# Adding an attention mask on VectorE instead of by a product on TensorE, from unit 12 of 24 on

## The chip, the cores and the metric

The kernel runs on one core of a Trainium2 chip. The metric is the time of one execution on the device in microseconds; a profiled execution also gives the span, from the first to the last instruction of the core. The engines are named as the profile names them: PE (TensorE, with its weight loads as PEld), DVE (VectorE), ACT (ScalarE), POOL (GpSimd) and SP (SyncE, which issues the transfers here).

## The reference

Three parts follow each other: a sparse attention, and two feed-forward layers on its output. All inputs and outputs are float32.

```python
def _attn_ref(q, k, v):                       # (2, 8, 768, 64) each
    k_sum = k.reshape(B, H, nb, 32, D).max(axis=3)
    v_sum = v.reshape(B, H, nb, 32, D).mean(axis=3)
    scores_l = scale * np.matmul(q, k.transpose(0, 1, 3, 2))
    mask_l = np.abs(pos[:, None] - pos[None, :]) < 16
    scores_s = scale * np.einsum('bhsd,bhnd->bhsn', q, k_sum) + np.log(32)
    scores_all = np.concatenate([np.where(mask_l, scores_l, -1e9), scores_s], axis=-1)
    a = softmax(scores_all)                   # written out, with 1e-9 in the divisor
    return np.matmul(a, np.concatenate([v, v_sum], axis=2))

def reference(...):
    x = attention, laid out as 1536 tokens x 512
    h = x @ w_in                              # 512 -> 2048
    x = (h * sigmoid(1.702 * h)) @ w_out      # 2048 -> 512
    return (sigmoid(x @ w_gate) * (x @ w_val)) @ w_out2   # 512 -> 1536 -> 512
```

Each token attends to the 31 tokens around it and to 24 block summaries; every other score is masked away.

## The kernel before

**Attention.** The work is cut into 24 units: 2 batches, 3 groups of four query blocks of 64 tokens, 4 pairs of heads. A unit's scores are a tile of 128 x 4 x 128: the rows are two heads by 64 queries, and each of the four blocks has 128 columns, of which the first 32 are block summaries and the other 96 the window. For unit `u`, `w_copy` scales the keys on POOL; `b_pe` (L553) fills one of three PSUM banks `ps_s` with first one product of `pick` and `mask` (L557, bf16, 512 columns), which lays the mask into the bank, and then four products of keys and queries (L559) accumulated on it; `b_max` (L562) takes the negated maximum of each block on VectorE (L564); `b_exp` (L567) makes four exponentials on ScalarE out of the bank into an SBUF tile `e`, with their sums. Then follow `n_inv` and `n_mul` (the division, VectorE and POOL), `c_pe` (four transposes of `e` into the bank `ps_p`, L592), `c_copy` (`pt`, out of that bank, L597, on ScalarE for the first ten units and on VectorE after them), `d_pe` (products with the values, L611), and `d_hi` and `d_lo`, which split the result into a high and a low float32r part. The pool of `e` has three buffers, that of `ps_s` three banks, `ps_p` one.

**Loop.** Step `t` of the loop at L703 issues `b_pe`, `b_max` and `b_exp` of unit `t`, `n_inv` and `n_mul` of unit `t - 1`, and `c_pe`, `c_copy` and `d_pe` of unit `t - 3`, in the order of the list `ORDER` (L638). Between them it issues transfers, sums for the second batch (`sum_v`, L521), pieces of weight decoding (`pull`, L102 to L112) and pieces of the first feed-forward layer for the tokens that are ready (`filler`). That layer has products into `ps_h`, a sigmoid on ScalarE (L373), a gating product on VectorE (L364), the split of its result into `gh` (ScalarE, L365) and `gl` (POOL, L366), and products into `ps_o` (all L349), accumulated by L425 or L429.

**Order.** Only SP runs in the order that the program writes down (`manual_schedule`). For the other engines a planner, which lays out a timeline with costs of its own (`schedule_with_timeline_sim`), decides the order of each engine's instructions, preferring what stands earlier in the program among what it holds to be ready. The engines then run in that fixed order and wait where they must.

**After the attention.** The rest of the two layers is a long run of 128x512 products on PE.

Of the kernel before, what the change touches and what calls it, by code (L numbers as in the profile page):

```python
# [8 lines left out]
F32 = mybir.dt.float32  # L9
# [4 lines left out]
ALU = mybir.AluOpType  # L14
AX = mybir.AxisListType
PSUM = bass.MemoryType.PSUM
P = 128
# [11 lines left out]
def attention_moe_moe2_kernel(ctx: ExitStack, tc: tile.TileContext, ins: dict, out: bass.AP):  # L29
    nc = tc.nc  # L30
# [13 lines left out]
    G = 4  # L44
    NG = NQB // G
    NTT = S // P
    NSLOT = G + NG - 1
# [120 lines left out]
    def load(slots, layer, g, i):  # L168
        raw, shape = raws.pop(0)
        hi, lo = (slots.tile(list(shape), F32R, name=f"w{layer}_{g}_{i}{x}") for x in "HL")  # L170
        parts = decode(raw, hi.rearrange("p a n -> p (a n)"), lo.rearrange("p a n -> p (a n)"))
        for step, _ in enumerate(parts):
            if step == 1 and (layer, g) != (1, 0):
                fetch()
            yield
        return hi, lo

    def load_group(layer, g):
        tiles = weights[layer, g] = []
        ready[layer, g] = 0  # L180
        for i in range(len(mats[layer])):
            tiles += yield from load(w_slots, layer, g, i)
            ready[layer, g] += 1
            yield
# [256 lines left out]
    acc_b = None  # L441
    EARLY = 4
    EARLY_UNITS = 10
    coming = (x for n in range(2) for x in load_group(*groups[n]))

    def pull(n):
        for _ in range(n):
            if next(coming, True):
                break
# [5 lines left out]
    with tc.manual_schedule(engines={mybir.EngineType.SP}), ExitStack() as es:  # L455
        one = es.enter_context(tc.tile_pool(name="a_one", bufs=1))
# [4 lines left out]
        ep = es.enter_context(tc.tile_pool(name="a_e", bufs=3))  # L461
        vp = es.enter_context(tc.tile_pool(name="a_v", bufs=1))
        ps_a = es.enter_context(tc.tile_pool(name="ps_a", bufs=1, space=PSUM))

        vwin = one.tile([P, 2 * G, H * D], F32, name="vwin")
        mask = one.tile([P, NSLOT, P], BF16, name="mask")
        pick = one.tile([P, P], BF16, name="pick")

        units = [(b, g, hp) for b in range(B) for g in range(NG) for hp in range(HP)]
        qbd, vsum, kraw, kmax, kx = {}, {}, {}, {}, {}  # L470
# [8 lines left out]
        def load_q(u, eng):  # L479

            b, g, hp = units[u]
            t = qp.tile([P, G, P], F32, tag="q", name=f"q{u}")
            eng.dma_start(out=t.rearrange("p i c -> p (i c)"), in_=q[b, g, hp])
            qbd[u] = t
# [32 lines left out]
        def sum_v(b, hp):  # L517
            if hp == 0:
                vpart[b] = vp.tile([P, HP, W0], F32, tag="vm", name=f"vm{b}")
                nc.vector.memset(vpart[b], 0.0)  # L520
            nc.vector.tensor_reduce(  # L521
                out=vpart[b][:, hp, 0:NB], in_=vtl.pop((b, hp)).rearrange("p (n t) -> p n t", t=BLK),
                axis=AX.X, op=ALU.add,
            )

        def sum_lay(b):
            r = vpart.pop(b)
            ps = ps_a.tile([W0, H * D], F32, tag="x", name="ps_v", bufs=2)
            for hp in range(HP):
                nc.tensor.matmul(ps[:, hp * P:(hp + 1) * P], lhsT=r[:, hp], rhs=ident, start=True, stop=True)  # L530
            nc.scalar.activation(vsum[b][0:W0], ps, AF.Copy, scale=1.0 / BLK)

        def prep_k(b, hp):
            ks = kp.tile([P, W0], F32, tag="ks", name=f"ks{b}_{hp}")
            nc.vector.memset(ks, 0.0)
            own = kraw[b, hp][:, HALO:HALO + S].rearrange("p (n t) -> p n t", t=BLK)
            nc.vector.tensor_reduce(out=ks[:, 0:NB], in_=own, axis=AX.X, op=ALU.max)
            kmax[b, hp] = ks
# [11 lines left out]

        live = {}

        def b_pe(u):  # L553
            b, g, hp = units[u]
            t, kt = qbd.pop(u), kx.pop(u)
            ps = ps_a.tile([P, G, P], F32, tag="s", name="ps_s", bufs=3)
            nc.tensor.matmul(ps, lhsT=pick, rhs=mask[:, g:g + G, :], start=True, stop=False)  # L557
            for j in range(G):
                nc.tensor.matmul(ps[:, j, :], lhsT=t[:, j, :], rhs=kt[:, j, :], start=False, stop=j == G - 1)  # L559
            live["s", u] = ps  # L560

        def b_max(u):  # L562
            nm = sp.tile([P, G], F32, tag="nm", name="nm")
            nc.vector.tensor_reduce(out=nm, in_=live["s", u], axis=AX.X, op=ALU.max, negate=True)  # L564
            live["nm", u] = nm

        def b_exp(u):  # L567
            s, nm = live.pop(("s", u)), live.pop(("nm", u))
            sm = sp.tile([P, G], F32, tag="sm", name="sm")
            e = ep.tile([P, G, P], F32, tag="e", name="e")  # L570
            for j in range(G):
                nc.scalar.activation(  # L572
                    e[:, j, :], s[:, j, :], AF.Exp, bias=nm[:, j:j + 1], accum_out=sm[:, j:j + 1]
                )
            live["e", u], live["sum", u] = e, sm
# [19 lines left out]
        def c_copy(u):  # L595
            t = sp.tile([P, G, P], F32, tag="pt", name="pt")
            (nc.scalar.copy if u < EARLY_UNITS else nc.vector.tensor_copy)(t, live.pop(("p", u)))  # L597
            live["pt", u] = t
# [49 lines left out]
        for _ in range(4):  # L648
            ps = ps_h.tile([P, TB], F32, tag="h", name="ps_w")
# [27 lines left out]
            out=win, in_=win, pattern=[[0, NSLOT], [1, P - W0]], compare_op=ALU.is_gt, fill=NEG,  # L677
# [3 lines left out]
            out=win, in_=win, pattern=[[0, NSLOT], [-1, P - W0]], compare_op=ALU.is_gt, fill=NEG,  # L681
# [21 lines left out]
        for t in range(-1, NU + LD):  # L703
            now[0] = t

            u = t + 2
            if u < NU and units[u][1] == 0:
                prep_k(units[u][0], units[u][2])
            for part, lag in ORDER:
                if 0 <= t - lag < NU:  # L710
                    part(t - lag)
            if 0 <= t < NU - 5:
                load_q(t + 5, nc.sync)
            if t == -1:
                sum_v(0, 0)
                sum_v(0, 1)
            if t == 0:
                sum_v(0, 2)
                sum_v(0, 3)
                sum_lay(0)  # L720
                load_v(0, 1)
                put_v(0, 1, nc.scalar)
                fetch()
            if t in (5, 8):
                fetch()
            if t in (7, 8, 9, 10):
                sum_load(1, t - 7)
            if t in (8, 9, 10, 11):
                sum_v(1, t - 8)
            if t == 11:  # L730
                sum_lay(1)

            if t % HP == HP - 1 and HP < t < NU - HP:
                c = t // HP + 1
                load_v(c // NG, c % NG)
                put_v(c // NG, c % NG)
            if 8 <= t < 8 + HP:
                load_k(1, t - 8)
            if t >= 1:
                pull(1 if t < 6 or t > 9 else 2)  # L740
            for _ in range(2 if t >= 8 else 1):
                next(fill, None)
# [3 lines left out]
    with tc.manual_schedule(engines={mybir.EngineType.SP}):  # L746
# [11 lines left out]
        for step in steps[EARLY:]:  # L758
            layer, g, blk = step
# [91 lines left out]
```

## Time and profile before

| | |
|---|---|
| median of 3 runs | 630.03 us (629.86 to 630.12) |
| the profiled execution | 629.99 us, its span 628.1 us |
| PE busy | 613.1 us, 98% of the span |
| VectorE busy | 430.8 us, 69% |
| ScalarE busy | 282.5 us, 45% |
| POOL busy | 194.8 us, 31% |
| granted clock of PE, mean | 0.997 |

Busy times are sums over the whole span. An engine with a low share can still be the one that sets the pace in one stretch. Records of PE's products overlap, so the distance from one start to the next tells what a product costs there, rather than the length of its record. In a timeline, the bracket at the end of a line is the time that the engine stood before that line and what ended the wait.

### The profile page before, as it was taken

To read this page: it belongs to the slowest core of one execution; us is meant where nothing else is said; L and a number is where in the kernel's file an instruction comes from. 1 tells how busy PE (TensorE), PEld (TensorE's weight loads), DVE (VectorE), ACT (ScalarE), POOL (GpSimd) and SP (SyncE) were. 2 spreads that over 40 slices of the span, in tenths; PEclk is the share of its full clock that TensorE was granted. 3 is DMA by queue.
4 is the path that set the end of the run, shared out by engine and by line. 5 is a ranking of instruction groups with operands and counts; after the bars stand their busy time and mean duration, and the time that the engine had idled before them with its cause. 6 is when DMAs were issued, how large, how long until landed. Compare 5 with 4: busy or idle time off the path is not lost.

```text
span 628.1 us, 8342 instructions
## 1 busy us (share of the span) xinstructions
PE 613.1 (98%) x3162; PEld 499.9 (80%) x3162; DVE 430.8 (69%) x628; ACT 282.5 (45%) x560; POOL 194.8 (31%) x164
## 2 busy tenths in 40 slices
PE   7898999999999999999999999999999999999997
PEld 4676787778888888888888887888887888888886
DVE  6699666488976665565379995279499479496524
ACT  4688657546443334232246645444344244333310
POOL 6797676233132313132222030120031120130210
PEclk9899999999999999999999999999999999999999
DMA  9997752044521222100001304012113012100004
GB/s 311 347 328 254 242 126 64 2 134 141 176 86 67 68 67 68 67 2 1 0 13 61 129 0 135 0 68 78 57 67 118 17 67 74 61 1 0 2 33 168
DMA packets 25160, 58.08 MB, mean 92 GB/s; under 512 B 1568, under 2 KB 1824, under 8 KB 25120
## 3 DMA queue, kind: packets, MB, share of 16 engines
q1 hardware_dynamic: 24400, 56.24, 27.6%
q10 hardware_dynamic: 720, 1.31, 0.6%
q8 instruction: 25, 0.41, 0.3%
q14 instruction: 15, 0.12, 0.1%
HBM read 53.08 MB, written 3.15 MB: 90 GB/s over the span
## 4 chain that ended last, share of the span: by engine, by line
PE 86%; DVE 9%; ACT 2%; issue 1%; DMA 1%; SPq 0%; DVEq 0%; ACTq 0%
PE ps_o L349 35%; PE ps_h L349 20%; PE ps_v L124 8%; PE ps_y L124 7%; PE ps_x L124 5%; PE ps_h L124 4%; PE ps_s L559 3%; PE ps_x L611 2%; PE ps_p L592 1%; DVE wf L205 1%; DVE ws L214 1%; DMA vt<-in_vt 1%; ACT e L572 1%; DVE nm L564 1%; DVE sg L364 1%
## 5 line engine op out<-in xcount | busy, mean ns | idle before, releaser
L366 POOL TENSOR_TENSOR gl<-sg,gh 128x512 fp32r<-128x512 f32 x84 | 119.5, 1424 | 393.7 <-ACT gh L365 372.0
L429 DVE TENSOR_TENSOR acc<-ps_o,acc 128x512 f32<-128x512 f32 x143 | 97.2, 686 | 56.9 <-PE ps_o L349 56.8
L365 ACT CAST gh<-sg 128x512 fp32r<-128x512 f32 x84 | 52.0, 620 | 89.8 <-DVE sg L364 79.6
L349 PE MATMUL ps_o<-gh,w_1L 128*128 128x512 f32 x192 | 74.5, 395 | 1.6 <-ACT gh L365 1.5
L349 PE MATMUL ps_h<-xH,w_0L 128*128 128x512 f32 x192 | 75.2, 396 | 0.5 <-DVE acc L429 0.5
L349 PE MATMUL ps_o<-gl,w_1H 128*128 128x512 f32 x192 | 75.4, 393 | 0.0
L349 PE MATMUL ps_h<-xL,w_0H 128*128 128x512 f32 x192 | 75.0, 391 | 0.0
L349 PE MATMUL ps_o<-gh,w_1H 128*128 128x512 f32 x192 | 74.8, 390 | 0.0
L349 PE MATMUL ps_h<-xH,w_0H 128*128 128x512 f32 x192 | 74.8, 390 | 0.0
L364 DVE TENSOR_TENSOR sg<-ps_h,sg 128x512 f32<-128x512 f32 x48 | 32.9, 687 | 44.1 <-ACT sg L373 43.8
L349 PE MATMUL ps_o<-w_2H,gl 128*128 128x512 f32 (+1 forms) x146 | 56.2, 388 | 1.0 <-ACT acc L425 0.6
L349 PE MATMUL ps_o<-w_2H,gh 128*128 128x512 f32 (+1 forms) x146 | 56.4, 386 | 0.0
L349 PE MATMUL ps_o<-w_2L,gh 128*128 128x512 f32 (+1 forms) x146 | 56.4, 386 | 0.0
L373 ACT ACTIVATE sg<-ps_h 128x512 f32<-128x512 f32 x48 | 28.3, 595 | 61.2 <-PE ps_h L349 61.2
L107 DVE SCALAR_TENSOR_TENSOR da<-da,db 128x1024 uint32<-128x1024 uint32 x34 | 43.9, 1290 | 14.4 <-ACT da L103 14.0
L103 ACT ACTIVATE da<-da 128x1024 f32<-128x1024 f32 x34 | 36.1, 1061 | 30.6 <-DVE da L102 28.6
L349 PEld LDWEIGHTS ps_o<-gh,w_1L 128*128 128x128 f32 x192 | 35.9, 188 | 9.3 <-ACT gh L365 2.0
L349 PEld LDWEIGHTS ps_h<-xH,w_0L 128*128 128x128 f32 x192 | 36.0, 188 | 8.2 <-DVE acc L429 0.9
L349 PEld LDWEIGHTS ps_h<-xH,w_0H 128*128 128x128 f32 x192 | 36.0, 188 | 7.6
L349 PEld LDWEIGHTS ps_o<-gh,w_1H 128*128 128x128 f32 x192 | 36.1, 188 | 7.3
L349 PEld LDWEIGHTS ps_o<-gl,w_1H 128*128 128x128 f32 x192 | 36.1, 188 | 7.3 <-POOL gl L366 0.2
L349 PEld LDWEIGHTS ps_h<-xL,w_0H 128*128 128x128 f32 x192 | 36.0, 188 | 7.4
(162 smaller groups left out, 1244.5 us busy)
## 6 DMA issues: line engine op xcount, KB each, us to landing
raw<-in_moe_w_out SPq DMA_DIRECT2D x13, 1024.0 KB, 4.9
raw<-in_moe_w_in SPq DMA_DIRECT2D x8, 1024.0 KB, 7.3
raw<-in_moe_w_gate SPq DMA_DIRECT2D x6, 1024.0 KB, 5.1
raw<-in_moe_w_val SPq DMA_DIRECT2D x6, 1024.0 KB, 5.1
q<-in_q SPq DMA_DIRECT2D x20, 256.0 KB, 7.5
vwin<-in_v SPq DMA_DIRECT2D x6, 768.0 KB, 8.1
k<-in_k SPq DMA_DIRECT2D x8, 400.0 KB, 6.5
out<-acc SPq DMA_DIRECT2D x11, 256.0 KB, 2.0
```

Source lines behind the costliest of these rows:

```text
L103: nc.scalar.activation(af, af, AF.Prelu, scale=REBIAS, alpha=-2.0 ** 32)
L107: nc.vector.scalar_tensor_tensor(out=a, in0=a, scalar=3, in1=b, op0=ALU.logical_shift_left, op1=ALU.bitwise_or)
L124: nc.tensor.matmul(ps, lhsT=a[x][:, kk, :], rhs=b[y][:, kk, :], start=start and i == 0, stop=i == n - 1, skip_group_check=True,)
L205: nc.vector.tensor_tensor(out=w.rearrange(flat), in0=hi.rearrange(flat), in1=lo.rearrange(flat), op=ALU.add)
L349: nc.tensor.matmul(ps, lhsT=a, rhs=b, start=i == 0, stop=i == n - 1)
L364: nc.vector.tensor_tensor(out=sg, in0=val, in1=sg, op=ALU.mult)
L365: nc.scalar.copy(gh, sg)
L366: nc.gpsimd.tensor_tensor(out=gl, in0=sg, in1=gh, op=ALU.subtract)
L373: nc.scalar.activation(sg, ps, AF.Sigmoid, scale=1.702 if layer == 1 else 1.0)
L429: nc.vector.tensor_tensor(out=a[:, m, :], in0=ps, in1=a[:, m, :], op=ALU.add)
L559: nc.tensor.matmul(ps[:, j, :], lhsT=t[:, j, :], rhs=kt[:, j, :], start=False, stop=j == G - 1)
L611: nc.tensor.matmul(ps[64 * e:64 * e + 64, j, :], lhsT=x[:, h * D:(h + 1) * D], rhs=y[:, j, 64 * e:64 * e + 64], start=n == 0, stop=n == le ...
```

## The change

For units 0 to 11 nothing changes. For the units from 12 on (`LATE = 12`) `b_pe` no longer issues the product of `pick` and `mask`; the four score products start their accumulation themselves. A new step `widen`, issued once at the end of step `t = 10`, makes the same product for all six mask slots (four, then two) into two score banks and copies it on ScalarE into a float32 tile `wide` in SBUF. For these units `b_max` first adds the bank and `wide` on VectorE into a tile `e`, and takes the maximum of that; `b_exp` reads `e` and writes the exponentials in place. So `e` is taken before the maximum instead of after it, and the score bank is read once, by the add.

```diff
+    LATE = 12
...
+        wide = one.tile([P, NSLOT, P], F32, name="wide")
...
+        def widen():
+
+            for a, b in ((0, G), (G, NSLOT)):
+                ps = ps_a.tile([P, G, P], F32, tag="s", name="ps_s", bufs=3)
+                ps = ps[:, 0:b - a, :]
+                nc.tensor.matmul(ps, lhsT=pick, rhs=mask[:, a:b, :], start=True, stop=True)
+                nc.scalar.copy(wide[:, a:b, :], ps)
+
         def b_pe(u):
...
-            nc.tensor.matmul(ps, lhsT=pick, rhs=mask[:, g:g + G, :], start=True, stop=False)
+            late = u >= LATE
+            if not late:
+                nc.tensor.matmul(ps, lhsT=pick, rhs=mask[:, g:g + G, :], start=True, stop=False)
             for j in range(G):
-                nc.tensor.matmul(ps[:, j, :], lhsT=t[:, j, :], rhs=kt[:, j, :], start=False, stop=j == G - 1)
+                nc.tensor.matmul(
+                    ps[:, j, :], lhsT=t[:, j, :], rhs=kt[:, j, :], start=late, stop=late or j == G - 1
+                )
             live["s", u] = ps
 
         def b_max(u):
+            if u >= LATE:
+                g = units[u][1]
+                e = ep.tile([P, G, P], F32, tag="e", name="e")
+                nc.vector.tensor_tensor(out=e, in0=live["s", u], in1=wide[:, g:g + G, :], op=ALU.add)
+                live["s", u] = e
             nm = sp.tile([P, G], F32, tag="nm", name="nm")
             nc.vector.tensor_reduce(out=nm, in_=live["s", u], axis=AX.X, op=ALU.max, negate=True)
             live["nm", u] = nm
...
-            e = ep.tile([P, G, P], F32, tag="e", name="e")
+            e = s if u >= LATE else ep.tile([P, G, P], F32, tag="e", name="e")
...
+            if t == LATE - 2:
+                widen()
```

## Rows read from the trace of the kernel before

**Rows 1.** The page, busy time of an engine, its share and instructions.
```profile
PE 613.1 (98%) x3162; PEld 499.9 (80%) x3162; DVE 430.8 (69%) x628; ACT 282.5 (45%) x560; POOL 194.8 (31%) x164
```
**Rows 2.** Three stretches: length, busy time (instructions) of each engine, clock, DMA share, GB/s.
```profile
36.00:46.60 10.60, 10.09 (x100) 8.25 (x100) 9.59 (x22) 9.49 (x34) 10.60 (x10) 1.00 1.02 307
46.60:64.10 17.50, 15.24 (x132) 10.63 (x131) 17.49 (x28) 15.24 (x47) 12.78 (x11) 1.00 0.71 239
64.10:106.00 41.90, 41.89 (x338) 34.21 (x339) 25.41 (x56) 27.07 (x91) 30.11 (x31) 1.00 0.57 162
```
**Rows 3.** The chain that ended last, in order of time: start, length, what.
```profile
46.61 0.69 DVE nm L564
...
63.28 0.68 DVE pt L597
...
64.10 0.69 PE ps_x L611 x16
```
**Rows 4.** The timeline of PE, from 57 to 103 us.
```profile
57.34 0.50 PE L349 MATMUL ps_o<-gh,w_1L 128*128 128x512 f32 x1 [1.50 <-ACT gh L365]
...
64.10 0.69 PE L611 MATMUL ps_x<-pt,vwin 128*64 128x64 f32 x16 [0.61 <-DVE pt L597]
...
65.71 0.38 PE L557 MATMUL ps_s<-mask,pick 128*128 128x512 bf16 x1
...
98.69 0.66 PE L592 MATMUL ps_p<-ident,e 128*128 128x128 f32 x4
...
100.65 0.71 PE L349 MATMUL ps_o<-gh,w_1L 128*128 128x512 f32 x2
...
102.57 0.38 PE L557 MATMUL ps_s<-mask,pick 128*128 128x512 bf16 x1
102.78 1.05 PE L559 MATMUL ps_s<-kx,q 128*128 128x128 f32 x8
```
**Rows 5.** The timeline of VectorE, from 56 to 66 us.
```profile
56.48 0.67 DVE L564 TENSOR_REDUCE nm<-ps_s 128x4 f32<-128x512 f32 x1
57.08 0.67 DVE L364 TENSOR_TENSOR sg<-ps_h,sg 128x512 f32<-128x512 f32 x1
...
58.27 1.45 DVE L112 TENSOR_TENSOR w_1L<-da,w_1H 128x1024 fp32r<-128x1024 f32 x1
...
61.76 0.67 DVE L564 TENSOR_REDUCE nm<-ps_s 128x4 f32<-128x512 f32 x1
...
65.91 0.69 DVE L564 TENSOR_REDUCE nm<-ps_s 128x4 f32<-128x512 f32 x1 [0.60 <-PE ps_s L559]
```
**Rows 6.** Groups by line: count, busy us, mean ns, idle before and releasers.
```profile
L429 DVE TENSOR_TENSOR acc<-ps_o,acc 128x512 f32<-128x512 f32 x143 | 97.2, 686 | 56.9 <-PE ps_o L349 56.8
L373 ACT ACTIVATE sg<-ps_h 128x512 f32<-128x512 f32 x48 | 28.3, 595 | 61.2 <-PE ps_h L349 61.2
L564 DVE TENSOR_REDUCE nm<-ps_s 128x4 f32<-128x512 f32 x24 | 16.2, 680 | 5.5 <-PE ps_s L559 5.4
L425 ACT COPY acc<-ps_o 128x512 f32<-128x512 f32 x24 | 13.7, 590 | 8.2 <-PE ps_o L349 8.0
L298 ACT ACTIVATE sg<-sg 128x512 f32<-128x512 f32 x12 | 7.6, 632 | 25.3 <-DVE sg L290 25.3
L537 DVE TENSOR_REDUCE ks<-k 128x24 f32<-128x768 f32 x8 | 7.5, 943 | 4.9 <-DMA k<-in_k 4.8
```
**Rows 7.** The timeline of ScalarE, from 93 to 100 us.
```profile
93.29 0.37 ACT L572 ACTIVATE e<-ps_s,nm 128x128 f32<-128x128 f32 x1 [0.34 <-PE ps_p L592]
...
99.07 0.62 ACT L365 CAST gh<-sg 128x512 fp32r<-128x512 f32 x1
```
**Rows 8.** The timeline of VectorE, from 94 to 106 us.
```profile
94.05 0.69 DVE L564 TENSOR_REDUCE nm<-ps_s 128x4 f32<-128x512 f32 x1
...
98.34 1.29 DVE L364 TENSOR_TENSOR sg<-ps_h,sg 128x512 f32<-128x512 f32 x2 [3.06 <-ACT sg L373]
...
105.32 0.68 DVE L564 TENSOR_REDUCE nm<-ps_s 128x4 f32<-128x512 f32 x1
```

## The prediction

> **What bounds the kernel now.** I read the busy times of the page first, then the same by stretches, then the chain of work that ended last, and last the timelines of PE and VectorE around the units that change. PE is busy for 98% of the span [rows 1], so one expects that less PE work is less time. The stretches show where this does not hold [rows 2]. From 64.10 to 106.00 us PE is busy 41.89 of 41.90 us, and VectorE only 25.41. From 46.60 to 64.10 us it is the other way round: VectorE 17.49 of 17.50 us, PE 15.24. The chain says the same [rows 3]: it runs over VectorE from 46.61 us on, nearly without a break, to the copy `pt` at 63.28, and passes to PE at 64.10, where PE had stood 0.61 us for that copy [rows 4]. Before that PE had stood 1.50 us at 57.34 [rows 4]. From 64.10 us on the chain is PE's.
>
> So the attention phase has a stretch that VectorE sets, followed by one that PE sets, and the change moves work from PE to VectorE in both. To sort the units: each has one maximum (L564), 24 in all. The last, unit 23's, starts at 105.32 us; counted back from there, unit 20's is at 94.05, and nine before the last stands unit 14's, at 65.91, with unit 13's at 61.76 and unit 12's at 56.48 [rows 5, 8]. Two of the twelve changed units thus have their maximum inside VectorE's stretch, ten after it.
>
> **What is removed.** Twelve mask products of 24 (L557). A record lasts 0.38 us, but matmuls overlap; what one costs is the distance to the next start: 102.57 to 102.78 us, 0.21 us [rows 4]. Twelve are 12 x 0.21 = 2.5 us of PE. Eight, those of units 16 to 23, start after 64.10 us (65.71 the first, 102.57 the last [rows 4]): 8 x 0.21 = 1.7 us where PE is never idle, so this comes off the end. The four of units 12 to 15 lie before that, in VectorE's stretch, where PE stands waiting anyway; I value them at nothing. If PE had no reason left to wait there they would be worth 4 x 0.21 = 0.8 us.
>
> **What is added, on PE and ScalarE.** `widen` issues two products of 512 and 256 columns: 0.21 + 0.11 = 0.32 us of PE, near unit 10 or 11, thus before 46.60 us. In 36.00 to 46.60 PE is busy 10.09 of 10.60 us [rows 2], so the 0.51 us idle can cover them: I take 0, with 0.32 as the other end. Of the two copies on ScalarE neither costs more than a 512-column copy out of a bank, 590 ns [rows 6]: at most 1.2 us together, and ScalarE has 10.60 - 9.49 = 1.1 us idle in that stretch [rows 2]. They take two places in the ring of three score banks. I take 0; without that cover they would push ScalarE's exponentials, and the maxima after them, by up to 1.2 us.
>
> **What is added on VectorE.** Twelve adds of 128x512 with one operand in a bank and one in SBUF. The nearest row is the accumulation `acc<-ps_o,acc`, the same shape and places, 686 ns [rows 6]. Back to back, VectorE starts instructions of 512 columns 0.60 us apart (56.48 and 57.08 [rows 5]), so an add costs 0.60 us of VectorE. The maximum that follows reads SBUF in place of the bank. A reduction from SBUF in the trace, 768 columns, takes 943 ns, 1.23 a column; that of 512 columns from the bank takes 680, 1.33 a column [rows 6]. Nothing there says that SBUF costs more, and I change nothing.
>
> For units 12 and 13 the adds fall at about 56.48 and 62.4 us, where VectorE has no gap. Everything behind them shifts: the second gate (57.08), pieces of weight decoding (58.27), and at 63.28 us the copy `pt` for which PE stands until 64.10 [rows 3 to 5]. Two adds make 2 x 0.60 = 1.2 us, and I take all of it on the path. The ends: 0, if the planner moves a decoding piece (1.45 us at 58.27 [rows 5]) behind that copy; 1.8, if unit 14's add comes in front of it as well. The ten later adds, 6.0 us, lie in stretches where VectorE has 41.90 - 25.41 = 16.5 us idle [rows 2]; I price them at 0. Without that cover the price is that of the rival on `e`, below.
>
> **Exponentials.** They now read SBUF. The nearest pair: a 128x512 sigmoid from SBUF takes 632 ns, from a bank 595 [rows 6], 37 ns more. Four to a unit, 48 in all: 1.8 us of ScalarE. For units 12 and 13 that is 8 x 37 ns = 0.3 us, in a stretch where ScalarE is idle for 17.50 - 15.24 = 2.3 us; for the later ones see the idle time in the last rival [rows 2]. I price all of it at 0, with 1.8 us as the end on the other side.
>
> [...]
>
> **Sum.** -1.7 (PE after 64.10) + 1.2 (VectorE before it) + 0 + 0 = -0.5 us. The profiled execution took 629.99 us, its span 628.1 and 1.89 around it; the median of the runs is 630.03, 0.04 above it. 629.99 - 0.5 = 629.5. A measurement here can tell a difference of about 0.2%, 1.3 us; the forecast lies inside that.
>
> **Rivals.**
> *The whole PE saving arrives.* The planner orders VectorE anew. If the decoding pieces, or the sums of `vt` (L521), which stand before the `pt` copy, go behind it, the 1.2 us disappear, and if PE has other work at 57.34 and 64.10 us, the four early products count too: 12 x 0.21 - 0.32 = 2.2 us, 627.8. Filling all of the 2.1 us that PE stood there would give 625.7. For it: the piece is there (1.45 us [rows 5]), and PE is short of nothing after 64.10. Against it: the trace shows that the order before did not do so, though the wait was there to be saved.
>
> *A wait for the buffers of `e` (slower).* The add writes into a buffer of `e`, of which there are three, so it can't start before the transposes (L592) of three units earlier have read theirs; before, only the exponential had to wait for that. The wait exists: before 93.29 us ScalarE had stood 0.34 us for it [rows 7]. Unit 20's maximum started at 94.05 us; the transposes of unit 17 start at 98.69 and last 0.66, to 99.35 [rows 8, 4]. In the same VectorE order the add would hold the engine until 99.35, and the two gates behind it, at 98.34 us [rows 8], would start at 99.35 + 1.2 = 100.55, 2.2 us late. Behind the gates are the cast at 99.07 [rows 7], the subtraction on POOL and the second products that PE starts at 100.65 [rows 4]. The cast ends at 99.69, 1.0 us ahead of them, so PE would stand from 1.2 to 2.2 us at this one place. At 2.2 us: 629.5 + 2.2 = 631.7. It decides against the kernel when PE's stand exceeds 1.8 us. Against it: the planner knows of the buffer and can put the gates in front of the add.
>
> *ScalarE's exponentials on the path (slower).* All 48 at 37 ns: 629.5 + 1.8 = 631.3. Against it: ScalarE is idle 14.8 of the 41.9 us after 64.10 [rows 2].
>
> **How the numbers follow.** The forecast (within 0.2%, 629.5, own range 628.8 to 631.2) gets 0.41; the whole PE saving 0.36, since nothing but the order keeps it away; the wait for `e` 0.17; the exponentials 0.06. Faster by over 0.2% is then 0.36, within 0.41, slower 0.23. The range goes from 627.2 (most of the second case) to 631.9 (a part of the wait for `e`).
>
> **What would show it.** The L557 group has 12 products of mask and pick on the old line and two on the new one; PE's busy time falls by about 2 us after 64 us and the phase up to the last attention product ends about as early as before. Twelve adds of about 0.69 us stand before the maxima. The exponentials from unit 12 on are some 40 ns longer than those before. VectorE is full up to the point where PE stops standing, and that point comes about 1.2 us later. If PE's idle time between 46 and 66 us has not grown, the second step of the sum is wrong and the time is near 627.8. If an add's wait on L592 stands among the long waits with a gate behind it, the rival on `e` holds. What I can't see in this trace is how far the planner's order of the other engines changes; a new standstill of PE over 2 us anywhere would make the forecast wrong.

## The result, and the profile after

The changed kernel takes 634.44 us (median of five runs, 632.54 to 636.44) against 630.03: a ratio of 1.0067, 95% interval 1.0052 to 1.0082, which is 3.3 to 5.2 us more. I had forecast 629.5 with a range up to 631.9. It is slower, and outside the range. The profiled execution took 632.54 us, its span 630.8; it is the fastest of the five, so its trace holds 2.6 of the 4.4 us. In `kernel.py` of the change the add is L580, the maximum L583, the exponentials L591, `rr` L600, `n_mul` L605, the copy `pt` L616, `d_pe` L630; the lines of the feed-forward layer are those of before.

The busy times of the page, beside [rows 1]:

```profile
PE 608.5 (96%) x3152; PEld 496.7 (79%) x3152; DVE 438.1 (69%) x640; ACT 284.2 (45%) x562; POOL 193.2 (31%) x164
```

PE has ten instructions less (twelve mask products gone, two of the widening new) and less busy time, yet the span is longer: PE stands more. The same three stretches as in [rows 2]:

```profile
36.00:46.60 10.60, 10.00 (x99) 7.93 (x99) 9.62 (x19) 9.48 (x34) 10.13 (x9) 1.00 1.05 287
46.60:64.10 17.50, 15.66 (x123) 11.82 (x123) 17.50 (x28) 12.69 (x32) 12.44 (x11) 1.00 0.76 246
64.10:106.00 41.90, 36.90 (x302) 30.79 (x301) 28.93 (x58) 27.54 (x92) 27.98 (x30) 1.00 0.56 161
```

The third line is the result. PE was busy 41.89 of 41.90 us there, and now is 36.90: it stands 5.0 us in the stretch where I had written that a product less comes off the end. VectorE, 28.93 of 41.90, is still far from full. Where PE stands from 46.60 to 145 us, in its timeline (of the lines left out none stood 0.2 us or more; the kernel before stood 1.50 and 0.61 us [rows 4], and 0.48 at 127.64):

```profile
55.76 0.73 PE L349 MATMUL ps_o<-gh,w_1L 128*128 128x512 f32 x2 [1.49 <-ACT gh L365]
...
73.31 2.05 PE L571 MATMUL ps_s<-kx,q 128*128 128x128 f32 x16 [1.17 <-POOL kx L550]
...
76.47 0.69 PE L630 MATMUL ps_x<-pt,vwin 128*64 128x64 f32 x16 [0.86 <-DVE pt L616]
...
85.75 0.50 PE L349 MATMUL ps_o<-gh,w_1L 128*128 128x512 f32 x1 [1.67 <-DVE acc L429]
...
101.65 0.91 PE L571 MATMUL ps_s<-kx,q 128*128 128x128 f32 x6 [0.90 <-issue]
102.84 0.73 PE L349 MATMUL ps_o<-gh,w_1L 128*128 128x512 f32 x2 [0.28 <-ACT gh L365]
...
119.95 0.73 PE L349 MATMUL ps_o<-gh,w_1L 128*128 128x512 f32 x2 [0.80 <-ACT gh L365]
...
135.45 0.50 PE L349 MATMUL ps_h<-xH,w_0L 128*128 128x512 f32 x1 [1.02 <-DVE sg L364]
```

No single wait is long. With one of 0.17 us at 61.10 they make 8.36 us after 46.60, against 2.59 before. The chain that ended last says how long the others now lead. It passed from VectorE to PE at 64.10 [rows 3]; now it does so at 85.75, after a transfer of weights, the decoding that waited for it, and the copy `pt` behind that (and it leaves PE again for ScalarE from 100.78 to 102.84):

```profile
67.43 6.86 DMA raw<-in_moe_w_out
...
74.31 1.50 DVE db L105
75.81 0.60 DVE pt L616
...
85.75 1.66 PE ps_o L349 x6
```

What leads to the first new stand for `kx`, at 73.31, begins in the stretch that VectorE sets. Its timeline there, beside [rows 5]:

```profile
55.57 0.68 DVE L580 TENSOR_TENSOR e<-ps_s,wide 128x512 f32<-128x512 f32 x1
56.17 0.68 DVE L616 COPY pt<-ps_p 128x512 f32<-128x512 f32 x1
56.77 0.86 DVE L105 TENSOR_SCALAR db<-raw 128x1024 uint32<-128x1024 uint32 x1
57.55 2.30 DVE L112 TENSOR_TENSOR w_1L<-da,w_1H 128x1024 fp32r<-128x1024 f32 x1
59.78 0.41 DVE L651 TENSOR_TENSOR xL<-ps_x,xH 128x256 fp32r<-128x256 f32 x1
60.11 0.94 DVE L523 TENSOR_REDUCE vm<-vt 128x24 f32<-128x768 f32 x1
60.97 0.67 DVE L583 TENSOR_REDUCE nm<-e 128x4 f32<-128x512 f32 x1
...
63.02 0.67 DVE L616 COPY pt<-ps_p 128x512 f32<-128x512 f32 x1
...
64.22 0.67 DVE L583 TENSOR_REDUCE nm<-e 128x4 f32<-128x512 f32 x1
```

The add of unit 12 starts at 55.57 us; its maximum, which I had thought of as the next instruction, at 60.97. The planner put five other instructions between them. Before, that maximum started at 56.48 [rows 5]: it is 4.5 us late, for an add of 0.60. Unit 13's maximum is 2.5 us late (64.22 against 61.76), while unit 11's copy `pt` is not late at all (63.02 against 63.28).

What this reaches is seen on POOL, which divides a unit (L605, L586 before) and scales keys (`kx`). First the kernel before, then the changed one:

```profile
65.06 2.04 POOL L586 TENSOR_TENSOR e<-e,rr 128x512 f32<-128x512 f32 x2 [1.08 <-DVE rs L579]
69.24 2.96 POOL L548 TENSOR_SCALAR kx<-k 128x384 f32<-128x384 f32 x2 [2.14 <-DMA k<-in_k]
72.18 1.02 POOL L548 TENSOR_SCALAR kx<-ks 128x128 f32<-128x128 f32 x2
```

```profile
66.11 1.04 POOL L605 TENSOR_TENSOR e<-e,rr 128x512 f32<-128x512 f32 x1 [2.99 <-DVE rr L600]
69.96 2.31 POOL L550 TENSOR_SCALAR kx<-k 128x384 f32<-128x384 f32 x2 [2.81 <-DMA k<-in_k]
72.23 1.03 POOL L550 TENSOR_SCALAR kx<-ks 128x128 f32<-128x128 f32 x2
73.22 2.04 POOL L605 TENSOR_TENSOR e<-e,rr 128x512 f32<-128x512 f32 x2
```

Before, units 12 and 13 are both divided from 65.06 on (x2), ahead of the scaling that waits for a load of keys. Now unit 13's division is no longer in time. It stands behind the scaling, which waits for the load, and starts at 73.22, 7 us late. The keys are ready at 73.2 us in both kernels; before, PE was busy to that point, now it has nothing left and stands 1.17 us for them. So a delay of a few us on VectorE seems to be turned into a longer one by a queue whose next place lies behind a transfer. This is read from two traces and accounts for one stand of 1.17 us; no run tests it by itself, and others lose their time without it (e14, below).

### The profile page after: what moved, and what is told of

Read it like the earlier page. It is cut to its first block, busy times and chain, and to the rows that moved or that the text cites. A ratio compares the mean times of both kernels' runs of the same rounds, so it can differ in the third digit from the quotient of the medians.

```text
span 630.8 us, 8337 instructions
## 1 busy us (share of the span) xinstructions
PE 608.5 (96%) x3152; PEld 496.7 (79%) x3152; DVE 438.1 (69%) x640; ACT 284.2 (45%) x562; POOL 193.2 (31%) x164
## 4 chain that ended last, share of the span: by engine, by line
PE 78%; DVE 10%; DMA 5%; ACT 4%; issue 2%; POOL 1%; SPq 0%; ACTq 0%; DVEq 0%
PE ps_o L349 34%; PE ps_h L349 17%; PE ps_v L124 8%; PE ps_y L124 7%; PE ps_x L124 5%; PE ps_h L124 4%; DMA xH<-in_moe_w_out 3%; ACT e L591 1%; DMA k<-in_k 1%; DMA raw<-in_moe_w_out 1%; DVE wf L205 1%; DVE ws L214 1%; DVE sg L364 1%; PE ps_s L571 1%; PE ps_x L630 1%
```

## The experiments

Times are medians; each ratio is to runs of the kernel before on the same chip, with its 95% interval.

| run | time, us | ratio |
|---|---|---|
| e1: the change again | 634.11 | 1.0082 (1.0058 to 1.0106) |
| e2: maximum of unit 12 behind its add | 634.89 | 1.0075 (1.0063 to 1.0088) |
| e3: the same, and a decoding piece behind `pt` | 632.80 | 1.0050 (1.0036 to 1.0064) |
| e4: `vs` stored from ScalarE's queue | 635.30 | 1.0086 (1.0072 to 1.0100) |
| e5: four buffers of `e` | 635.66 | 1.0087 (1.0074 to 1.0100) |
| e6: add in place, in the bank | 635.39 | 1.0082 (1.0069 to 1.0095) |
| e7: removal alone | 629.17 | 0.9989 (0.9981 to 0.9998) |
| e8: e5 and e3 together | 633.94 | 1.0065 (1.0052 to 1.0078) |
| e9: adds alone, zeros filled at the start | 633.23 | 1.0054 (1.0041 to 1.0067) |
| e10: adds beside, zeros filled at the start | 632.82 | 1.0048 (1.0034 to 1.0061) |
| e11: widening alone | 629.51 | 0.9995 (0.9984 to 1.0005) |
| e12: from unit 20 on | 630.16 | 1.0003 (0.9995 to 1.0012) |
| e13: adds alone, no fill | 636.82 | 1.0109 (1.0094 to 1.0124) |
| e14: adds beside, no fill | 636.28 | 1.0102 (1.0088 to 1.0115) |
| e15: units 12 to 15 only | 633.04 | 1.0057 (1.0043 to 1.0071) |
| e16: from unit 16 on | 629.85 | 1.0003 (0.9994 to 1.0011) |
| e17: from unit 14 on | 632.33 | 1.0040 (1.0027 to 1.0054) |
| e18: two copies `pt` to ScalarE | 634.93 | 1.0083 (1.0070 to 1.0096) |

**The order (e1 to e4).** e1 is the change unaltered. My first theory was the order: the add torn from its maximum delays `vs`, and behind that SP's queue of loads.

> The changed kernel as it is, again, to see its spread beside the others. All theories: 632.5 to 636.4 us, as in its first five runs; a spread of several us, where the kernel before spreads over 0.3.

e2 and e3 add dependences without a semaphore, which only tell the planner what comes behind what: in e2 four instructions that stood between add and maximum come behind the maximum, in e3 also a decoding piece behind the copy `pt` for which PE stood 0.86 us.

```diff
+    marks = {}
+
+    def behind(ins, key):
+
+        if key in marks:
+            tc.add_manual_dep(
+                ins.ins, marks[key].ins.name,
+                mybir.DependencyInfo(mybir.DependencyClass.NoSync, mybir.DependencyReason.DATA), reason="behind",
+            )
+
+    BEHIND = {('pt', 10): ('max', 12), ('tail', (1, 2, 0)): ('max', 12), ('low', (1, 1, 1)): ('max', 12), ('low', 9): ('max', 12)}
...
```

This is e2; in e3 the dictionary has one entry more, `('tail', (1, 2, 1)): ('pt', 12)`. `tail` is the decoding piece L105, `low` is L112 or `d_lo`. For e4:

```diff
-                put_v(c // NG, c % NG)
+                put_v(c // NG, c % NG, nc.scalar if c == NG else nc.sync)
```

> The changed kernel with the order of VectorE mended in one place: unit 12's maximum comes right behind its add and one sum of vt; the copy pt of unit 10, two pieces of decoding and one xL go behind it. Theory Q (queue): the maximum, torn from its add, came 5.4 us late, with it the exponentials and the copy of vs on ScalarE, and on SP's queue the loads of keys and weights behind the transfer of vs. Then the maximum starts near 57 us instead of 61, the transfer of vs near 63 instead of 64.8, and the time falls by 1 to 3 us, to 631 to 632.5. Theory W (work): it is the adds' own 0.6 us each that VectorE can't hide, in whatever order: no change, 633 to 635. Theory E (buffers of e): no change either.

> The edit of the kernel before it in this call, and the decoding piece that waits for the weights loaded behind vs goes behind unit 12's copy pt, as it stood before the change. Theory Q: PE's wait of 0.86 us for pt at 76.5 us is gone too, and the time is 0.5 to 1.5 us below that of the first edit alone: 629.5 to 631.5. Theories W and E: 633 to 635.

> The changed kernel, with only the transfer of the second batch's sums vs issued from ScalarE's queue instead of SP's, so that the loads of keys and weights behind it don't wait for vs. Theory Q: the loads go out near 52 instead of 65 to 68 us, PE's waits at 73.3 and 76.5 us (1.17 and 0.86) vanish, and the time falls to 629 to 632. Theory W: the adds still cost the same, 633 to 635. Theory E: 633 to 635.

e2 brought the maximum to 1.5 us behind the add and gained nothing. In e4, which takes the store of `vs` out of SP's queue, the load of keys goes out at 53.74 us instead of 65.51 and POOL no longer waits for it, and nothing is gained either. e3 is the fastest of the whole-change variants, and still 2.3 to 4.0 us slower than before. Why e2 and e3 help so little is not shown. The planner ordered POOL anew too (here e3's timeline): now unit 12's division stands behind the load as well, at 69.95, and unit 13's at 73.75. Yet PE has no stand for `kx` there any more; it stands in other places.

```profile
68.82 1.18 POOL L566 TENSOR_SCALAR kx<-k 128x384 f32<-128x384 f32 x1 [4.66 <-DMA k<-in_k]
69.95 1.70 POOL L621 TENSOR_TENSOR e<-e,rr 128x512 f32<-128x512 f32 x1
...
73.75 1.03 POOL L621 TENSOR_TENSOR e<-e,rr 128x512 f32<-128x512 f32 x1
```

SP's queue as the cause of the whole loss falls by e4. But no run here moves one thing alone, for the planner orders ScalarE anew as well. Where ScalarE passes from exponentials to sigmoids or back, its timeline has an `ACT_TABLE_LOAD` of 1.28 us; the kernel before and the change have eight of them in all, e2, e3, e4, e7, e8 and e15 ten, e5 and e6 twelve. What one engine's order costs I could not separate.

**The buffers of `e` (e5, e6, e8).** This is the prediction's rival. Adds do wait for the transposes in the changed kernel, 3.3 us in three waits. The first edit is that of e5 and e8 (e8 has e3's order as well), the second that of e6, where the exponentials then take a tile `e` as before.

```diff
-        ep = es.enter_context(tc.tile_pool(name="a_e", bufs=3))
+        ep = es.enter_context(tc.tile_pool(name="a_e", bufs=4))
...
-                e = ep.tile([P, G, P], F32, tag="e", name="e")
-                nc.vector.tensor_tensor(out=e, in0=live["s", u], in1=wide[:, g:g + G, :], op=ALU.add)
-                live["s", u] = e
+                e = live["s", u]
+                nc.vector.tensor_tensor(out=e, in0=e, in1=wide[:, g:g + G, :], op=ALU.add)
```

> The changed kernel with four buffers of e instead of three. Theory E (buffers of e): in the changed kernel the add takes its buffer before the maximum, and from 100 us on it waits for the transposes of three units earlier; the bank it would empty stays full, and PE waits (0.90 at 101.7 us, 0.80 at 120.0). With a fourth buffer the adds' waits on the transposes (3.3 us in the changed kernel) are gone, unit 23's exponentials end before 112 us instead of at 116.6, PE's waits at 101.7 and 120.0 are gone, and the time falls by 1.5 to 3 us, to 631 to 632.5. Theory Q (queue): nothing changes before 90 us, 633 to 635. Theory W (work): 633 to 635.

> The changed kernel, but the add writes its sum back into the score bank and the exponentials read the bank and write e, so that e is taken as late as before the change. Theory E: as with a fourth buffer the adds wait no longer, and the time falls by 1.5 to 3 us, to 631 to 632.5. Theory W: the adds still cost 0.6 us of VectorE each, 633 to 635. If the price lies in the exponentials' source (bank 0.34, SBUF 0.39 us each), this gives back the 0.04 us times 48 on ScalarE as well.

> Four buffers of e, and the two mends of VectorE's order of the second and third kernel (maximum near its add; the piece behind unit 12's copy). Theory E with a part for Q: both gains add up, 629 to 631, level with the kernel before or below. Theory W: VectorE's 0.6 us per add stays, 632 to 634.

In e5 and e6 no add waits for a transpose any more, and PE's stand of 0.90 us at 101.65 is gone with it; others came in its place, 1.03 us at 106.89 in e5 and 1.55 us at 107.40 in e6, both for a gate. The time is 4.3 to 6.3 us above before in both. The rival's wait was there, and taking it away in these two ways gains nothing. What it costs by itself stays open, since both runs also have four table loads more, 5.1 us of ScalarE. e8, with e3's order as well, stays 3.3 to 4.9 us above before.

**Removal, adds, widening (e7, e9 to e11, e13, e14).** Each part by itself. In e7 the units from 12 on have neither mask product nor add, and there is no widening:

```diff
-            if u >= LATE:
-                g = units[u][1]
-                e = ep.tile([P, G, P], F32, tag="e", name="e")
-                nc.vector.tensor_tensor(out=e, in0=live["s", u], in1=wide[:, g:g + G, :], op=ALU.add)
-                live["s", u] = e
...
-            e = s if u >= LATE else ep.tile([P, G, P], F32, tag="e", name="e")
+            e = ep.tile([P, G, P], F32, tag="e", name="e")
...
-            if t == LATE - 2:
-                widen()
```

> The mask products of units 12 to 23 are left out and nothing is put in their place: no widen, no add (so the scores of these units are not masked). All theories: this is what PE gets back, 12 times 0.21 us where PE is the bound. If the eight products after 64 us count, 628.2; if all twelve, 627.4. If the planner's new order alone does the harm, it may show here too, at 630 or more, since the order changes here as well.

PE's saving, 12 x 0.21 = 2.5 us, comes back as 0.8 us (0.1 to 1.2), even with nothing added. The stands of PE after 46.60 make 4.22 us in this run, 1.6 more than before, with new ones for `kx`, for copies `pt` and for a gate: with less to do PE reaches its waits sooner, and the order of the other engines is a new one here too.

> The kernel before with the widening at the end of step 10 (two mask products, two copies on ScalarE) and nothing that reads it. By V (the widening shifts the order of everything from unit 10 on, or holds two score banks) 632 us or more. By W, C and P 629.5 to 630.5 us; my prediction priced it at 0, with 0.3 of TensorE and 1.2 of ScalarE as the other end.

The widening at step 10, as in the change, with nothing that reads it (`LATE = 24`), costs nothing.

e9, e10, e13 and e14 keep every mask product (the first edit). In e9 and e10 the added tile is of zeros, filled on VectorE at the start (the second), and there is no widening. In e10 and e14 the add is replaced by one beside the unit's way (the third).

```diff
-            late = u >= LATE
+            late = False
...
+        nc.vector.memset(wide, 0.0)
...
+                side = sp.tile([P, G, P], F32, tag="side", name="side")
+                nc.vector.tensor_tensor(out=side, in0=live["s", u], in1=wide[:, g:g + G, :], op=ALU.add)
```

> All 24 mask products stay on TensorE, there is no widen, and the units from 12 on still add a tile on VectorE (a tile of zeros, filled once at the start, so the scores are those of the kernel before) and take maximum and exponentials from the sum in SBUF. This is the added VectorE work alone. The removal alone gave -0.8 us and the whole change +3.3 to +4.4. If the adds cost the time (theory W, the work on VectorE, or C, the longer way of each unit), this kernel stands at 633 to 636 us, since -0.8 has to be taken off to come to the whole change. If the loss needs TensorE to run ahead of the others, because it has less to do (theory P), it stands at 630 to 631 us. If the widening is what costs (theory V), within 1 us of the kernel before.

> As the run with the adds alone, but the add of the units from 12 on comes after the maximum and writes into a tile that nobody reads; maximum and exponentials are taken from the bank as in the kernel before. VectorE has the same twelve instructions more, but no unit's way from scores to division is longer, and the exponentials read the bank. By W (the engine's time is what counts) 632 to 635 us, like the adds alone. By C (the way of each unit counts: an add of 0.69 us and slower exponentials ahead of every transposition) 629.5 to 631 us.

Both lost 2 to 4 us, which seemed to confirm the adds. But the fill delays the mask itself, and with it the first units (PE's timeline of e9; before, PE stood 0.7 us for the mask):

```profile
6.32 1.44 PE L569 MATMUL ps_s<-mask,pick 128*128 128x512 bf16 x3 [3.27 <-POOL mask L700]
```

So I repeated them with the widening of the change in place of the fill.

> The change with all 24 mask products kept: the widening as in the change, twelve adds, exponentials from SBUF, and nothing filled at the start. The mask is counted twice for the units from 12 on (so the summaries weigh more there). By W or C (the adds cost it, whatever TensorE does) 633 to 635 us. By P (the loss needs TensorE to have run ahead and to wait) at most 631 us. If the first run with the adds alone lost its time only by the fill at the start, 630 to 631 us as well; then the sum of removal and adds does not give the whole, and the loss comes from the two together.

> As the run before in the list, but the adds write into a tile that nobody reads, after the maximum; nothing is counted twice, and maximum and exponentials read the bank. By W 632.5 to 635 us. By C (the way of each unit) or P 630 to 631 us.

Without the fill the cost is larger, not smaller: the adds alone cost 5.9 to 7.8 us, more than the whole change. Why the runs with the fill lost less is not settled; one part may be the clock, since the profiled execution of e9 has no fall of it after 48 us and that of e13 has one (0.86 and 0.72 in the stretches of 4 us from 56 on). As a bare sum, removal and adds would make 7.3 - 0.8 = 6.5, not the 4.4 measured: by the medians the removed products are worth 2.9 us when the adds are there and 0.8 when they are not. By the intervals that is 0.7 to 4.5 and 0.1 to 1.2, so a difference between the two is not shown. The adds whose result nobody reads (e14) cost about as much, 5.5 to 7.2 us, with exponentials that read the bank. So the loss needs neither the slower exponentials nor scores that are ready later by one add; what e13 and e14 share is twelve instructions more in VectorE's order (and the widening, which alone costs nothing). The place where it is lost is not the same. In e14 units 12 and 13 are divided ahead of the scaling, and PE never stands for `kx` after 60 us; its longest stand, 2.41 us, is for exponentials that come behind a table load. POOL, ScalarE and PE of e14:

```profile
67.68 1.04 POOL L604 TENSOR_TENSOR e<-e,rr 128x512 f32<-128x512 f32 x1 [2.42 <-ACT vs L533]
71.17 1.84 POOL L604 TENSOR_TENSOR e<-e,rr 128x512 f32<-128x512 f32 x1 [2.45 <-DVE rr L599]
72.98 2.31 POOL L550 TENSOR_SCALAR kx<-k 128x384 f32<-128x384 f32 x2
...
102.42 1.28 ACT L590 ACT_TABLE_LOAD   x1
...
105.27 0.38 PE L569 MATMUL ps_s<-mask,pick 128*128 128x512 bf16 x1 [2.41 <-ACT e L590]
```

**Which units (e12, e15, e16, e17).** `LATE` is set to 20, 16 and 14; in e15 the new path is taken for `LATE <= u < 16` alone.

> The whole change from unit 20 on: four adds instead of twelve, the widening at the end of step 18, all of it after 80 us, where VectorE is idle a third of the time. By the sum of my prediction (adds after 64 us cost nothing) 4 x 0.21 - 0.32 = 0.5 us less than before, 629.5. By W or C with each add worth as much as another, a third of +3.3 to +4.4: 631.0 to 631.5 us. If only the adds up to 64 us cost (units 12 and 13), 629 to 630 us.

> The change for units 12 to 15 alone; from 16 on the mask is a product again. By my prediction (two adds in the stretch that VectorE sets cost 1.2 us, the removed products there are worth nothing) 631.2 us. If these four carry the whole loss, 633 to 635 us; if each add costs as much as another (a third), 631.0 to 631.5 us; if the later ones carry it, 630 us.

> The whole change from unit 16 on: eight products removed, eight adds, none of them in the stretch that VectorE sets. By my prediction (1.7 us of TensorE off, adds covered by idle time) 628.6 us. If units 12 to 15 carry the loss, 629 to 630 us. If the adds of units 16 to 19 do, 632 to 634 us. If each add costs as much as another, 632.2 to 632.9 us.

> The whole change from unit 14 on: ten products removed, ten adds, none of those of units 12 and 13, the widening at the end of step 12. If the adds of units 12 and 13 carry the loss, as those that stand in the stretch that VectorE sets, 629.5 to 630.5 us, as from unit 16 on. If units 14 and 15 carry it, 632.5 to 634 us. If each of the four carries a quarter, 631.5 to 632 us.

Units 12 to 15 alone cost 3.5 us (2.7 to 4.5), units 16 to 23 alone 0.3 (-0.4 to 0.7); together 3.8, about the whole. Units 20 to 23 alone (e12) come to 0.1 (-0.3 to 0.8). e15's POOL timeline has the divisions of units 13 and 14 together behind the scaling, at 74.60 (x2), with PE standing 1.19 us for `kx` at 74.69, while e16 has units 12 and 13 divided together at 65.30, as before. In e16 the eight removed products (1.7 us) bring nothing, and PE's timeline and VectorE's show where a part of it may have gone:

```profile
100.84 0.69 PE L630 MATMUL ps_x<-pt,vwin 128*64 128x64 f32 x16 [0.73 <-DVE pt L616]
...
107.41 0.69 PE L630 MATMUL ps_x<-pt,vwin 128*64 128x64 f32 x16 [0.90 <-DVE pt L616]
```

```profile
99.51 0.68 DVE L580 TENSOR_TENSOR e<-ps_s,wide 128x512 f32<-128x512 f32 x1
100.11 0.68 DVE L616 COPY pt<-ps_p 128x512 f32<-128x512 f32 x1
...
106.07 0.69 DVE L580 TENSOR_TENSOR e<-ps_s,wide 128x512 f32<-128x512 f32 x1 [0.81 <-PE ps_o L349]
106.68 0.68 DVE L616 COPY pt<-ps_p 128x512 f32<-128x512 f32 x1
```

VectorE is idle a third of this stretch, and yet an add stands directly in front of the copy for which PE waits, twice. The adds alone can't be blamed for all of it: with no add at all, in e7, PE stands for two such copies as well, 0.53 us at 81.38 and 0.68 at 106.65.

e17 leaves units 12 and 13 as they were and still loses 1.7 to 3.4 us. Its trace shows another wait: the widening, at step 12 now, falls into the full stretch, and `gh` starts at 60.35, against 56.65 in the trace of before. The widening's two copies put 0.72 us on ScalarE, from their starts to the next; the rest is order, for `gh` now stands behind a table load (57.41, 1.28 us) and a unit's exponentials, which came after it before. ScalarE's timeline of e17:

```profile
51.47 0.61 ACT L561 COPY wide<-ps_s 128x512 f32<-128x512 f32 x1
...
56.07 0.38 ACT L561 COPY wide<-ps_s 128x256 f32<-128x256 f32 x1
...
60.35 1.16 ACT L365 CAST gh<-sg 128x512 fp32r<-128x512 f32 x2
```

PE stands 2.23 us for it. Its stands, three of 0.17 to 0.38 us from 55.77 to 58.16 and those of 2.23 and 0.63 us at 61.05 and 62.41, are followed by a lower granted clock (stretches of e17, clock in the third column from the end):

```profile
60.00:64.00 4.00, 2.33 (x7) 1.60 (x8) 4.00 (x8) 1.97 (x7) 2.93 (x3) 0.89 0.06 19
64.00:68.00 4.00, 4.00 (x40) 2.40 (x39) 0.78 (x5) 2.63 (x10) 3.04 (x4) 0.69 0.18 36
```

So e17 can't say what the adds of units 14 and 15 cost.

**Relief of VectorE (e18).**

```diff
-    EARLY_UNITS = 10
+    EARLY_UNITS = 12
```

> The whole change, and the copies pt of units 10 and 11 are made by ScalarE instead of VectorE: 2 x 0.60 us off VectorE at 56.17 and 63.02 us, as much as the adds of units 12 and 13 put on it. If VectorE's time in that stretch is what costs, the loss goes: 629.5 to 631 us. If it is the longer way of units 12 and 13, or the planner's other order of them, it stays at 633 to 635 us.

No gain (4.4 to 6.0 us above before). In its trace the first add starts at 58.18 and the maximum at 63.58, again with four instructions between, and units 13 and 14 are divided together behind the scaling at 76.40. Taking off as much VectorE time as the adds put on does not bring the order back, so the loss does not seem to be that amount of time as such; but the two copies now take ScalarE's time (620 ns at the median for the copies `pt` that it makes in the changed kernel), and e18 does not separate that.

**An account.** For each profiled execution I added what PE's stands after 46.60 us grew by, the PE work taken off (0.21 us a mask product) or put on (0.32, the widening, an estimate: 0.21 and half of it), and the slow clock ((1 - granted clock) x length, from stretches of 4 us after 48 us):

| run | stands | work | clock | sum | measured, against 629.99 |
|---|---|---|---|---|---|
| the change | +5.8 | -2.2 | 0 | +3.6 | +2.6 |
| e7 removal | +1.6 | -2.5 | 0 | -0.9 | -1.0 |
| e13 adds | +5.4 | +0.3 | 1.7 | +7.4 | +7.9 |
| e15 units 12 to 15 | +3.2 | -0.5 | 0 | +2.7 | +2.4 |
| e16 from 16 | +1.3 | -1.4 | 0 | 0.0 | +0.1 |
| e17 from 14 | +2.5 | -1.8 | 1.7 | +2.4 | +2.2 |
| e3 order | +4.2 | -2.2 | 1.7 | +3.7 | +3.9 |

It closes to within 1.1 us for these and for nine more. In e5, e8 and e18 it falls short, by 1.6 to 3.5 us; e5 has a stretch of lower clock at 36 to 44 us (0.76, 0.81) and e8 stands 1.6 us more before 46.60, which this sum leaves out. The start differs between the traces of before and after, too: before, the clock was 0.50 from 18 to 20 us and 0.69 from 20 to 22, in the change 1.00, and unit 11's maximum starts at 46.61 us before and at 46.10 now. That may be a part of the 1.0 us by which the row of the change misses. So the sum says that the loss is PE standing, and in some executions its clock; it doesn't say which order made each stand.

## Why the prediction was wrong, point by point

**What bounds the kernel.** Right as read: VectorE fills 46.60 to 64.10 us in both kernels (17.50 of 17.50 now). That from 64.10 on the chain is PE's was right of the kernel before, but it did not carry over to the changed one. PE was always busy there because others had kept it supplied, barely: e7 takes work from PE alone, and 1.6 of 2.5 us turn into waits.

**The removal (-1.7).** This step failed. The size of a product holds. That it comes off the end because PE is never idle there does not: all twelve bring 0.8 us where nothing is added (e7), and the rest turns into new waits.

**The widening (0) and the exponentials (0).** The widening held: e11 is within 1.0 us below and 0.3 above before. The exponentials' price was not tested by itself. The first and the fourth exponential of a unit from SBUF and from the bank, in ScalarE's timeline (the changed kernel, then the kernel before):

```profile
67.23 0.40 ACT L591 ACTIVATE e<-e,nm 128x128 f32<-128x128 f32 x1
...
68.39 0.39 ACT L591 ACTIVATE e<-e,nm 128x128 f32<-128x128 f32 x1
```

```profile
62.89 0.34 ACT L572 ACTIVATE e<-ps_s,nm 128x128 f32<-128x128 f32 x1
...
63.92 0.34 ACT L572 ACTIVATE e<-ps_s,nm 128x128 f32<-128x128 f32 x1
```

Three steps take 1.16 us and 1.03 us: 43 ns more for each in these two units, where I had taken 37. The rival on the exponentials falls as the cause of the loss, with e14: they read the bank there, and 6.7 us are lost.

**Two adds in VectorE's stretch (1.2).** This step failed, in its path and in its size. The length of an add held (680 ns at the median, 0.60 from start to start), but "Two adds make 2 x 0.60 = 1.2 us, and I take all of it on the path" takes the order as given and adds a length to it. The sign that I had named for this step speaks against it: PE's idle time from 46 to 66 us did not grow, it fell from 2.27 to 1.84 us, and the copy `pt` of 63.28 starts at 63.02. The planner did put other work behind that copy, as my first rival had it. But the time did not come near 627.8, as I had concluded, for the work that was put off came back later: unit 12's maximum 4.5 us late, unit 13's 2.5, unit 13's division 7 us late, and PE's new stands from 73 us on. Units 12 to 15 alone cost 3.5 us where my sum had 1.2. I had named the planner as what I couldn't see; I had not given it a price on the slow side.

**Ten later adds (0).** From unit 16 on I had -1.7 and 0, and the runs show +0.3, so 2.0 us are missing there. A part is the removal's, which brings at most 1.2 us even alone. The rest comes with the adds: idle time summed over 41.9 us (16.5 us) was no sure cover, for in e16's rows an add stands in front of a copy for which PE waits, twice. How the 2.0 us divide is not measured.

By units the misses add up: 3.5 - 1.2 = 2.3, and 0.3 + 1.7 = 2.0; 4.3 of the 4.9 us by which the median (634.44) missed the forecast. By parts the adds are the larger miss: 7.3 us alone (e13) where I had 1.2, the removal -0.8 (e7) where I had -1.7. These two make 6.5, more than the whole change, so the parts do not simply add.

**The rivals.** The whole saving does not arrive, not even with no add at all (e7). The buffers of `e` made their wait, but the two kernels without it gain nothing (e5, e6), with other orders on ScalarE as well. A rival was missing: that PE stands in many places for under 2 us each. My last warning, a standstill of over 2 us, would not have caught it; the longest new one is 1.67. The sign on the end of the phase did speak: the last product with the values starts at 128.54 us, against 123.99 before.

**What stays open.** How the 3.5 us of units 12 to 15 divide between the two pairs, since e17 lost its time elsewhere; and which engine's order makes the loss. That the adds make it is shown (e13 and e14 against e11 and e7); that they do so through the planner's new orders is argued from the traces, since every variant changed the orders of several engines at once. A run with the order of VectorE, POOL and ScalarE held as before, and the adds put in, would settle it. No variant that keeps the mask was faster than the kernel before by more than the noise, and the removal alone brought 0.8 us: in these orders there was little to win.

## What to carry to other kernels

Before pricing work that goes to an engine with much idle time, look at what stands next in that engine's order and who waits for it: in e16 two adds of 0.6 us stood in front of copies for which PE then stood 0.73 and 0.90 us, on an engine idle a third of the time. Where a planner makes the order, an added instruction is an added degree of freedom, and a forecast needs a price on the slow side for a new order. A variant that changes one line changes the orders too: count what else moved, such as eight table loads becoming twelve, before it is read as a test of one cause. And measure the removal by itself: if it brings a third of what its instructions take, PE's full busy share was not a bound but a balance.

## What the runs showed of the hardware

In some executions of the variants the clock that TensorE is granted fell after a stand of PE; in others it stayed at 1.00 after one as long. In e2 PE stood 1.49 us up to 58.65 us, and the two stretches of 4 us from 56 on had a granted clock of 0.86 and 0.71; in the profiled execution of the change PE stood as long up to 55.76, and the clock stayed at 1.00, as it did in the kernel before after its 1.50 us [rows 4], and in e16 after 1.72 us at 57.58.

```profile
56.00:60.00 4.00, 2.38 (x25) 1.80 (x23) 4.00 (x9) 2.64 (x4) 3.94 (x5) 0.86 1.00 261
60.00:64.00 4.00, 4.00 (x17) 3.11 (x17) 4.00 (x6) 3.30 (x10) 2.32 (x2) 0.71 0.12 33
64.00:68.00 4.00, 4.00 (x34) 3.15 (x33) 3.17 (x8) 2.32 (x6) 0.53 (x1) 1.00 0.61 144
```

By the account above one such fall costs 0.14 x 4 + 0.29 x 4 = 1.7 us. It may be part of why the changed kernel's runs spread from 632.5 to 637.7 us: the six runs of it and of e1 with a mean clock of 0.999 or 1.000 took 632.5 to 634.4 us, the five with 0.992 to 0.997 took 634.5 to 637.7. The stand of about 1.5 us near 57 us is not new. New ones were followed by a fall as well: in e4 one of 1.92 us at 80.84 (0.87 and 0.71 in the two stretches from 80 on), in e14 that of 2.41 us at 105.27 (0.77 and 0.80 from 104 on). So in these executions a stand was followed by a second loss, as clock; whether the stand makes it is not shown, since no run tests that by itself. The measured median can hold both, while a trace at 1.00, as that of the change, holds only the first.
